# Strassen's form in the second product for four pairs of a chunk instead of two, in a kernel of channel attention and a gated network

## The chip, the cores and the metric

The program runs on one core of a Trainium2 chip. What is measured is device time in microseconds (us) of one execution; lower is better. Each engine of the core has an instruction stream of its own: PE (TensorE, the matrix products), ACT (ScalarE), DVE (VectorE), POOL (GpSimd) and SP, whose queue here issues nearly all DMAs. PSUM has 8 banks of 128 partitions by 512 float32; the products land there.

## The reference

For each of 4 batches, q, k and v are 6080 x 256. The columns of q and k are normed over the 6080 rows, a 256 x 256 attention between channels is formed, and `v @ a` goes through a network with 2048 hidden units.

```python
qn = q / (np.linalg.norm(q, axis=1, keepdims=True) + 1e-06)
kn = k / (np.linalg.norm(k, axis=1, keepdims=True) + 1e-06)
s = kn.transpose(0, 2, 1) @ qn / tau
a = np.exp(s - s.max(-1, keepdims=True))
a /= a.sum(-1, keepdims=True) + 1e-09
x = (v @ a).astype(np.float32).reshape(B * S, D)
h = x @ w_in
g = h * (1.0 / (1.0 + np.exp(-1.702 * h)))
return (g @ w_out).astype(np.float32)
```

## The kernel before

The kernel folds the attention of a batch into the network's first matrix (`a @ w_in`, once a batch), so that per token only two products are left: the **first product** (256 inputs to 2048 hidden units) and, behind the gate, the **second product** (2048 hidden units back to 256 outputs). Tokens lie along the free axis. A batch's 6080 tokens are cut into 6 **chunks**, five of 1024 and one of 960 columns; each has a left and a right half of 512 (or 480) columns. There are 24 chunks in all. Odd batches run their chunks backwards.

The 2048 hidden units are 8 **pairs** of 2 x 128. One pair in one chunk is a **unit** (`unit`); 192 units. To keep float32's accuracy with the fast float32r matmuls every operand is split into a high and a low part, and every product of two blocks is three matmuls: high x high, high x low, low x high. The split is a cast on ACT (`cast`, L299) or on DVE (`cast_v`, L302) and a subtraction on DVE (`low`, L310). Other two-operand work on DVE is `tt` (L305).

The first product of a unit is a 2x2 block product (two blocks of inputs, two of hidden units, two halves of columns) in Strassen's form (Winograd's variant): 7 block products of 3 matmuls, 21 instead of 24. They go to the banks X (two in turn), Y and Z, and copies on ACT and sums on DVE put the results together (`snap`, `add`, L966 for the matmuls). The gate (`gate`, L982) is on ACT.

The second product of a unit is done in one of two ways. **Plain** (L1046): the gated halves h1 and h2 are split (`split`: two casts and two lows of 1024 columns) and 8 block products, 24 matmuls, are added up in four banks O0 to O3 over the pairs of the chunk. **Joint** (`Joint`, L904), for two pairs (6 and 7, `MS = PAIRS = 2`), in each chunk but the first: the gates of both pairs write to tiles `g_a` and `g_b`, four sums of 1024 columns are formed on DVE (t1, t2, t3, t4), seven parts are split (7 casts, 7 lows of 1024 columns), and 7 block products of 2 pairs x 3 matmuls, 42 instead of 48, go to O0, O1 and O2. O1 is used for four products in turn (P1, P6, P5, P3); between them ACT copies what it holds to the output tile `osb` (`snap` in `products`). A split part is held in one of four tiles `gh` with its `gl` (`gh_slot`), taken in turn by the order in which the code asks for them, by joint parts and plain splits alike. The weights of the joint products are formed once and loaded again in each chunk as `w_oj`, four loads; the plain ones as `w_o`; both share four tiles (`NWO = 4`). The first product's weights `w_op` (896 KB a unit) have three. `values` splits a chunk's v into seven operands `v_op` of 512 columns; three of them (P1, P2, P6) have two tiles, the others one.

In the first chunk of a batch, and all through batches 0 to 2, the next batch's attention is worked in: loads of q and k, squares (ACT) and their sums `acc` (DVE), split of q and k (`qks`), the scores (PE, 256 columns), and at the end of the batch the next weights. The last batch has none of it.

What sets the order: `Plan` collects all instructions with dependencies, a cost, and a due time (45 units of time for each unit, plus an offset from the table `DUE` for its kind), runs a list scheduler over the engines, and emits the instructions in the order that comes out. Each engine then works through its own list strictly in that order.

In the joint chunks the pairs run in the order 6, 7, 0, 1, 2, 3, 4, 5:

```python
            joint = b > 0 or c > 0
            p = (x - MS) % NU if joint else x
```

## Time and profile before

| | |
|---|---|
| median of 3 runs (lowest, highest) | 2142.53 us (2141.75, 2144.03) |
| the profiled execution | 2142.41 us |
| its span, first to last instruction | 2140.6 us |
| TensorE clock granted, mean | 0.998 of full |
| busy: PE, DVE, ACT | 2131.3, 1659.3, 1409.6 us |
| matmul records, DVE and ACT instructions | 9774, 2199, 2078 |
| DMA | 448.32 MB, 209 GB/s over the span |

The profile is of one execution. Busy time of an engine is the time in which at least one of its instructions ran; matmuls overlap, so the mean duration of one (388 ns) is longer than the distance from one to the next. "PEld" is the load of weights, which runs beside the matmuls. In the lists of waits, the engine named first waited for the one behind the arrow. Some matmul records can be missing.

### The profile page before, as it was taken

The page shows a single profiled execution, that of the slowest core. Times are in us where ns is not written, and L with a number is a line of the kernel's source. Part 1 is how long each engine was busy: PE and PEld are TensorE (multiplying, and loading weights), DVE is VectorE, ACT ScalarE, POOL GpSimd, SP SyncE. Part 2 cuts the span into 40 slices and gives each one's busy share as a digit, 9 for nine tenths or more (in the row PEclk, how much of TensorE's full clock was granted, in tenths as well). Part 3 has the DMA queues.
Part 4 walks back from the last instruction along what each step waited for, and adds up shares of the span by engine and source line. Part 5 has one row for each costly group of instructions (what it writes and reads, how often), then busy time and mean ns, then how long its engine had stood idle before and what let it go on. Part 6 is the DMA issues. An engine that isn't in the chain of part 4 may idle for free.

```text
span 2140.6 us, 26818 instructions
## 1 busy us (share of the span) xinstructions
PE 2131.3 (100%) x9774; PEld 1785.7 (83%) x9774; DVE 1659.3 (78%) x2199; ACT 1409.6 (66%) x2078; POOL 6.4 (0%) x10
## 2 busy tenths in 40 slices
PE   9999999999999999999999999999999999999999
PEld 8888888888888888888888888888888888888887
DVE  6898888787778787867888878787787676676664
ACT  5568777666667676666766667666676565665663
POOL 0000000000000000000000000000000000000000
PEclk9999999999999999999999999999999999999999
DMA  9867666656765555555676556555577554554541
GB/s 342 307 216 284 236 246 217 218 176 219 258 243 200 188 204 192 207 172 180 245 255 211 189 197 211 182 202 173 183 251 256 187 201 150 201 180 160 195 170 74
DMA packets 124099, 448.32 MB, mean 209 GB/s; under 512 B 13120, under 2 KB 17344, under 8 KB 123968
## 3 DMA queue, kind: packets, MB, share of 16 engines
q1 hardware_dynamic: 123824, 446.48, 59.3%
q8 instruction: 77, 1.26, 0.2%
q14 instruction: 54, 0.44, 0.1%
q10 hardware_dynamic: 144, 0.13, 0.0%
HBM read 385.22 MB, written 61.34 MB: 209 GB/s over the span
## 4 chain that ended last, share of the span: by engine, by line
PE 98%; DMA 1%; ACT 0%; SPq 0%; issue 0%; DVE 0%; ACTq 0%
PE ps_o L1046 37%; PE ps_X L966 24%; PE ps_Y L966 12%; PE ps_o L904 10%; PE ps_Z L966 6%; PE ps_s L535 4%; PE ps_s L541 3%; PE ps_w L718 2%; DMA out_T<-osb 1%; DMA raw_qk<-in_q 0%; PE ps_n L595 0%; ACT osb L299 0%; PE ps_t L667 0%; SPq L296 0%; ACT gh L299 0%
## 5 line engine op out<-in xcount | busy, mean ns | idle before, releaser
L1046 PE MATMUL ps_o<-gh,w_o 128*128 128x512 f32 (+1 forms) x2336 | 716.6, 388 | 0.0
L966 PE MATMUL ps_X<-v_op,w_op 128*128 128x512 f32 (+1 forms) x2304 | 628.8, 389 | 0.6 <-ACT u L299 0.6
L1046 PEld LDWEIGHTS ps_o<-gh,w_o 128*128 128x128 f32 x2336 | 436.7, 188 | 86.8
L966 PEld LDWEIGHTS ps_X<-v_op,w_op 128*128 128x128 f32 x2304 | 430.3, 188 | 88.1 <-ACT u L299 1.4
L310 DVE TENSOR_TENSOR gl<-h,gh 128x1024 fp32r<-128x1024 f32 (+1 forms) x292 | 354.2, 1213 | 149.0 <-ACT gh L299 137.8
L1046 PE MATMUL ps_o<-gl,w_o 128*128 128x512 f32 (+1 forms) x1168 | 452.7, 388 | 0.0
L299 ACT COPY s<-ps_X 128x512 f32<-128x512 f32 (+1 forms) x384 | 222.7, 580 | 215.4 <-PE ps_X L966 142.3
L966 PE MATMUL ps_Y<-v_op,w_op 128*128 128x512 f32 (+1 forms) x1152 | 322.6, 388 | 0.0
L982 ACT ACTIVATE h<-h 128x512 f32<-128x512 f32 (+3 forms) x292 | 240.0, 838 | 58.8 <-DVE h L305 58.4
L1046 PEld LDWEIGHTS ps_o<-gl,w_o 128*128 128x128 f32 x1168 | 219.2, 188 | 43.9
L966 PEld LDWEIGHTS ps_Y<-v_op,w_op 128*128 128x128 f32 x1152 | 214.9, 188 | 42.8 <-DVE h L305 0.8
L904 PE MATMUL ps_o<-gh,w_oj 128*128 128x512 f32 (+1 forms) x644 | 222.2, 388 | 1.2 <-ACT osb L299 1.2
L299 ACT COPY u<-ps_X 128x512 f32<-128x512 f32 (+1 forms) x192 | 111.1, 578 | 119.3 <-DVE h L305 70.1
L299 ACT CAST gh<-h 128x1024 fp32r<-128x1024 f32 (+1 forms) x154 | 160.5, 1042 | 38.6 <-PE ps_o L904 25.7
L966 PE MATMUL ps_Z<-v_op,w_op 128*128 128x512 f32 (+1 forms) x576 | 161.0, 388 | 0.0
L302 DVE CAST gh<-h 128x1024 fp32r<-128x1024 f32 (+1 forms) x138 | 94.5, 685 | 80.5 <-PE ps_o L1046 59.1
L904 PEld LDWEIGHTS ps_o<-gh,w_oj 128*128 128x128 f32 x644 | 120.9, 188 | 26.6 <-ACT osb L299 2.5
L305 DVE TENSOR_TENSOR h<-ps_Y,s 128x512 f32<-128x512 f32 (+1 forms) x146 | 99.3, 680 | 44.8 <-ACT s L299 35.9
L305 DVE TENSOR_TENSOR h<-ps_Z,s 128x512 f32<-128x512 f32 (+1 forms) x146 | 99.2, 680 | 37.6 <-ACT s L299 17.2
L305 DVE TENSOR_TENSOR acc<-acc,sq 128x1024 f32<-128x1024 f32 (+2 forms) x96 | 112.8, 1175 | 18.4 <-ACT sq L502 16.6
L966 PEld LDWEIGHTS ps_Z<-v_op,w_op 128*128 128x128 f32 x576 | 107.7, 188 | 21.2
L904 PE MATMUL ps_o<-gl,w_oj 128*128 128x512 f32 (+1 forms) x322 | 124.8, 388 | 0.0
(110 smaller groups left out, 2281.3 us busy)
## 6 DMA issues: line engine op xcount, KB each, us to landing
w_op<-w_ops SPq DMA_DIRECT2D x184, 896.0 KB, 5.3
w_o<-wo_ops SPq DMA_DIRECT2D x138, 512.0 KB, 3.6
w_oj<-wj_ops SPq DMA_DIRECT2D x69, 512.0 KB, 3.8
raw_qk<-in_q SPq DMA_DIRECT2D x114, 256.0 KB, 5.4
raw_qk<-in_k SPq DMA_DIRECT2D x114, 256.0 KB, 5.5
w_ops<-w_op SPq DMA_DIRECT2D x32, 896.0 KB, 5.5
v_raw<-in_vT SPq DMA_DIRECT2D x20, 1024.0 KB, 6.8
out_T<-osb SPq DMA_DIRECT2D x39, 512.0 KB, 5.5
```

Source lines behind the costliest of these rows:

```text
L299: return g.add("ACT", act(n, psum), lambda: nc.scalar.copy(dst(), src()), deps, uses, due)
L302: return g.add("DVE", dve_fast(n), lambda: nc.vector.tensor_copy(dst(), src()), deps, uses, due)
L305: return g.add("DVE", dve(n), lambda: nc.vector.tensor_tensor(dst(), a(), b(), op=op), deps, uses, due)
L310: lambda: nc.vector.tensor_tensor(dst(), src(), hi().bitcast(F32), op=ALU.subtract),
L535: nc.tensor.matmul(out, lhsT=hl()[:pp, 1, j, ci], rhs=hl()[:pp, 0, j, :], start=begin, stop=last, skip_group_check=True,)
L541: nc.tensor.matmul(out, lhsT=hl()[:pp, 1, j, l, ci], rhs=hl()[:pp, 0, j, r, :], start=begin and m == 0, stop=last and m == 2, skip_group_c ...
L718: nc.tensor.matmul(pb()[:, x * width : (x + 1) * width], lhsT=aT()[:, l, j, ci], rhs=wi()[:, r, o : o + width], start=x == 0 and n == 0, s ...
L904: nc.tensor.matmul(of(into), lhsT=wt()[:, x, j, l, :], rhs=r()[:, j, :hw], start=begin and j == 0 and n == 0, stop=True, skip_group_check= ...
L966: nc.tensor.matmul(of(into), lhsT=wt()[:, m, l, :], rhs=v[m]()[:, r, :hw], start=begin and n == 0, stop=True, skip_group_check=True,)
L982: "ACT", act(n, psum), lambda: nc.scalar.activation(dst(), src(), AF.Gelu_apprx_sigmoid),
L1046: nc.tensor.matmul(of(ob), lhsT=wo()[:, l, i, ds], rhs=rr()[:, n * hw : (n + 1) * hw], start=first and m == 0, stop=True, skip_group_check ...
```

## The change

Four pairs (4 to 7) go in the joint form instead of two, as two groups of two pairs: group `b` in the table's names is pairs 6 and 7 (index 1), group `a` is pairs 4 and 5 (index 0). Each group has its own `g_a` and `g_b`; the products of both groups for one block are added in the same bank, so that each chunk has 14 parts, 8 sums and 84 joint matmuls, and 4 plain units. This holds from the third chunk of batch 0 on; the second chunk has the joint form for pairs 6 and 7 alone, as before, and the weights for pairs 4 and 5 are formed in it (`wout_later`, from a copy `wout_f` in DRAM). The joint pairs run first (4, 5, 6, 7, then 0 to 3). The weights `w_oj` come in seven loads of 512 KB, one for each block product, through the same four tiles. Of the plain units all four have the cast of h2 on DVE (before: all six); all joint casts are on ACT. `values` splits blocks of v that lie side by side together: P1 with P2, P5 with P7, P4 with P3, as one cast and one low of 1024 columns each (P6 alone); now only the first pair has two tiles. To make room, some tiles share a place that had one each: `wst`, `t2` and the words of small statistics go to `wa`, `sq` and one tile `few`, and the store of the next batch's weights is two DMAs instead of one. Every number of `DUE` is new, so the order of instructions changes everywhere.

```diff
 DUE = {
-    "m1": -16, "s1": -89, "m2": 50, "m6": 44, "u2": -64, "c11": -4, "g11": 193, "m5": 58, "u4": -39,
...
+    "m1": 17, "s1": -290, "m2": 48, "m6": 58, "u2": -133, "c11": -41, "g11": 708, "m5": 62, "u4": -220,
+    "m7": 67, "c22": -175, "m3": -16, "g12": -259, "m4": 71, "c21": -85, "g2": 1066, "h1": -392, "l1": 6,
...
 LAG = 3200
 NWO = 4
+MS = 4
+NV = {"m1": 2}
+NH = 2
+BY_V = (4, 5, 6, 7)
 
...
-    MS = PAIRS
     JOINT = list(range(NU - MS, NU))
-    wo_ops = dr.tile([NU - MS, P, 2, 2, C], F32, name="wo_ops")
-    wj_ops = dr.tile([P, NK, MS, 2, P], F32, name="wj_ops")
+    JG = MS // PAIRS
+    wo_ops = dr.tile([NU, P, 2, 2, C], F32, name="wo_ops")
+    wout_f = dr.tile([P, FG * C], F32, name="wout_f")
+    wj_ops = dr.tile([NK, P, MS, 2, P], F32, name="wj_ops")
...
+        if grp == NG - 1:
+            wout_sevens(grp, t, n, due + DUE["wj"], "acc")
+        elif PAIRS * grp in JOINT:
+            wo_stored["f"] = g.add("SP", 50 + 512 * 2.6, lambda: nc.sync.dma_start(wout_f, t()), [n], [t], due + 20, lag=LAG)
         return got
+
+    def wout_sevens(grp, t, ready, due, sums):
+
+        for a in range(PAIRS):
+            p = PAIRS * grp + a
+            view = lambda i, a=a: lambda: t()[:, (2 * a + i) * C : (2 * a + i + 1) * C].rearrange("p (d x) -> p d x", d=2)
+            wo_stored["joint", p] = sevens(
+                (t, view(0)), (t, view(1)), [ready], due + 20 * a, [("gA0", 0, NK)], sums,
+                lambda k, z, p=p: wj_ops[k:z, :, p - JOINT[0]].rearrange("k p h x -> p k h x"),
+            )[2]
+
+    def wout_later(grp, due, after):
+        t = sbuf("gB0", [P, FG * C], F32, "wf")
+        n = load(lambda: t(), wout_f, 512, [wo_stored["f"], *after], [t], due - 25)
+        wout_sevens(grp, t, n, due, "w1")
...
-    def wout_joint(due):
+    def wout_joint(due, pairs):
         got = {}
-        stored = [wo_stored["joint", p] for p in JOINT]
-        for x, (k, z) in enumerate(((0, 2), (6, 7), (4, 6), (2, 4))):
-            w = wo_tile([P, 2, MS, 2, P], "w_oj")
-            n = load(lambda w=w, k=k, z=z: w()[:, : z - k].bitcast(F32), wj_ops[:, k:z], 256 * (z - k), stored, [w], due + 8 * x)
-            for m in range(k, z):
-                got[m] = w, m - k, n
+        first = pairs[0] - JOINT[0]
+        stored = [n for p in pairs for n in wo_stored["joint", p]]
+        for x, m in enumerate((P1, P2, P6, P7, P5, P3, P4)):
+            w = wo_tile([P, MS, 2, P], "w_oj")
+            got[m] = w, load(
+                lambda w=w: w()[:, first:].bitcast(F32), wj_ops[m][:, first:], 128 * len(pairs), stored, [w], due + 8 * x,
+            )
         return got
...
-            v = sbuf(f"v{m}{turn if m in TWICE else ''}", [P, 2, HALF], F32R, "v_op")
-            at_ = due + 36 * n if m in TWICE else use + DUE[what] - 20
-            h = cast(lambda v=v: v()[:, 0, :hw], src, hw, [dep], [use_, v], at_)
-            ok[m] = low(
-                lambda v=v: v()[:, 1, :hw], src, lambda v=v: v()[:, 0, :hw], hw, [h], [use_, v], at_ + 6,
-            )
-            out[m] = v
...
+        def part(ms, what, src, n, deps, use_, at_):
+
+            k = len(ms)
+            v = sbuf(f"v{what}{turn % NV.get(what, 1)}", [P, 2, k, HALF], F32R, "v_op")
+            hi, lo = (lambda h=h: v()[:, h, :, :hw] if k > 1 else v()[:, h, 0, :hw] for h in range(2))
+            h = cast(hi, src, k * hw, deps, [use_, v], at_)
+            l = low(lo, src, hi, k * hw, [h], [use_, v], at_ + 6)
+            for i, m in enumerate(ms):
+                out[m] = v, lambda r, i=i, v=v: v()[:, r, i, :hw]
+                ok[m] = l
+            return l
+
+
+        col = lambda: raw()[:, :, :hw]
+        row = lambda j: lambda: raw()[:, j, : 2 * hw].rearrange("p (a n) -> p a n", a=2)
+        l1 = part((P1, P2), "m1", col, hw, [r], raw, due)
+        t1 = tt(B(0, 0), B(0, 1), B(0, 0), ALU.subtract, hw, [r, l1], [raw], due + 60)
+        t2 = tt(T2, B(1, 1), B(0, 0), ALU.subtract, hw, [t1], [raw, vt], due + 70)
+        t3 = tt(B(0, 1), B(0, 1), B(1, 1), ALU.subtract, hw, [t1], [raw], due + 80)
+        t4 = tt(B(1, 0), B(1, 0), T2, ALU.subtract, hw, [t2, l1], [raw, vt], due + 90)
+        part((P6,), "m6", T2, hw, [t2], vt, use + DUE["m6"] - 20)
+        part((P5, P7), "m5", row(0), hw, [t1, t3], raw, use + DUE["m5"] - 20)
+        part((P4, P3), "m3", row(1), hw, [t4], raw, use + DUE["m3"] - 20)
         return out, ok
...
+        def __init__(self, x, pairs):
+            self.x, self.pairs, self.ready = x, pairs, []
+            self.A = sbuf(f"gA{x}", [P, 2, len(pairs), HALF], F32, "g_a")
+            self.B = sbuf(f"gB{x}", [P, 2, len(pairs), HALF], F32, "g_b")
+
+    def joint_products(groups, b, c, due, wo):
...
+        for G in groups:
+            G11, G12, G2 = ([r[i] for r in G.ready] for i in range(3))
+            l1 = part(G, P1, "1", block(G.A, 0), G11, G.A)
+            l2 = part(G, P2, "2", block(G.B, 0), G2, G.B)
+            sums_[G.x] = G11, G12, G2, l1, l2
+        for G in groups:
...
+            t2 = sbuf("sq", [P, m_, HALF], F32, "g_t")
...
+            t1 = tt(B11, B12, B11, ALU.subtract, n_, [*G12, l1], [A], at("ta", G.x))
+            t2n = tt(T2, B22, B11, ALU.subtract, n_, [t1, *G2], [A, B_, t2], at("tb", G.x))
+            part(G, P6, "6", T2, [t2n], t2)
+            t4 = tt(B21, B21, T2, ALU.subtract, n_, [t2n, l2], [B_, t2], at("td", G.x))
+            t3 = tt(B12, B12, B22, ALU.subtract, n_, [t1, *G2], [A, B_], at("tc", G.x))
+            sums_[G.x] = G2, t1, t3, t4
+        for m, what, tile_, i, dep in (
+            (P7, "7", "A", 1, 2), (P5, "5", "A", 0, 1), (P3, "3", "B", 1, 0), (P4, "4", "B", 0, 3),
+        ):
+            for G in groups:
+                t = getattr(G, tile_)
+                dep_ = sums_[G.x][dep]
+                part(G, m, what, block(t, i), dep_ if isinstance(dep_, list) else [dep_], t)
+
...
+        def product(m, what, into, begin, deps):
+            ns = []
+            wt, w_ok = wo[m]
+            for G in groups:
+                gh, gl, ok = parts_[m, G.x]
+                m_ = len(G.pairs)
+
+                def fn(G=G, gh=gh, gl=gl, m_=m_):
                     for j in range(m_):
                         for n, (l, r) in enumerate(((0, gh), (0, gl), (1, gh))):
                             nc.tensor.matmul(
-                                of(into), lhsT=wt()[:, x, j, l, :], rhs=r()[:, j, :hw],
-                                start=begin and j == 0 and n == 0, stop=True, skip_group_check=True,
+                                of(into), lhsT=wt()[:, PAIRS * G.x + j, l, :], rhs=r()[:, j, :hw],
+                                start=begin and G is groups[0] and j == 0 and n == 0, stop=True, skip_group_check=True,
                             )
 
...
+                ns.append(g.add(
+                    "PE", 3 * m_ * width_cost(hw), fn, [*deps, ok, w_ok, *ns], [gh, gl, wt, into], at("q" + what, G.x), kind=hw,
+                ))
+            return ns[-1]
+
...
         r1 = split(h1, [g11, g12], "1", cast)
-        r2 = split(h2, [g2], "2", cast if D < NU else cast_v)
+        r2 = split(h2, [g2], "2", cast_v if D >= NU and x % NU in BY_V else cast)
...
-            joint = b > 0 or c > 0
-            p = (x - MS) % NU if joint else x
+            joint = JOINT if b > 0 or c > 1 else JOINT[-PAIRS:] if c > 0 else []
+            order = joint + [p for p in range(NU) if p not in joint]
+            p = order[x]
             grp, a = divmod(x, PAIRS)
...
             if joint and x == 0:
-                J = Joint(JOINT)
-                wj = wout_joint(due + DUE["wa"])
-            if joint and x >= MS:
+                Js = []
+                wj = wout_joint(due + DUE["wa"], joint)
+            if x < len(joint) and a == 0:
+                Js.append(Joint((p - JOINT[0]) // PAIRS, [p, p + 1]))
+            if joint and p not in joint:
                 wos[p] = wout_again(p, due + DUE["wb"])
-            unit(W, V[b, c], b, c, p, x, None if joint and x < MS else wos[p], J if joint and x < MS else None)
-            if joint and x == MS - 1:
-                J.products(b, c, due, wj)
+            unit(W, V[b, c], b, c, p, x, None if p in joint else wos[p], Js[-1] if p in joint else None)
+            if b == 0 and c == 1 and x == 3:
+                wout_later(JOINT[0] // PAIRS, due + 20, [marks[-1]])
+            if joint and x == len(joint) - 1:
+                joint_products(Js, b, c, due, wj)
...
```

How the order moves is shown at three places, all in the last batch's third chunk or, for the queue of DMAs, its last. `gh`, `gl` are a part's high and low half, `w_oj` the weights of joint products, `ps_o`, `ps_X`, `ps_Y`, `ps_Z` the banks.

PE, before: what stands between the last plain product of the chunk before and the joint product P7, whose part takes over the same `gh` and `gl` tile (the first row reads the old part, the last one the new one).

```order
L1046 MATMUL ps_o_15575<-gl_15859,w_o_15691 128x512
L966 MATMUL ps_X_16012<-v_op_15213,w_op_15948 128x512 x3
L904 MATMUL ps_o_16021<-gh_15906,w_oj_15771 128x512
L904 MATMUL ps_o_16021<-gl_15918,w_oj_15771 128x512
L904 MATMUL ps_o_16021<-gh_15906,w_oj_15771 128x512 x2
L904 MATMUL ps_o_16021<-gl_15918,w_oj_15771 128x512
L904 MATMUL ps_o_16021<-gh_15906,w_oj_15771 128x512
L966 MATMUL ps_Y_15993<-v_op_15779,w_op_15786 128x512 x3
L966 MATMUL ps_X_15940<-v_op_15264,w_op_15863 128x512 x3
L966 MATMUL ps_Z_16044<-v_op_15220,w_op_15863 128x512 x3
L904 MATMUL ps_o_16049<-gh_16028,w_oj_15937 128x512
```

Between these two rows stand 18 matmuls.

PE, after: what stands between the product P2 of the second group and P7 of the second group, whose part takes over P2's tile (neither is in the rows).

```order
L1015 MATMUL ps_X_16169<-v_op_15804,w_op_16072 128x512 x3
L1015 MATMUL ps_X_16250<-v_op_15297,w_op_16166 128x512 x3
L950 MATMUL ps_o_16118<-gh_16134,w_oj_16053 128x512
L950 MATMUL ps_o_16118<-gl_16138,w_oj_16053 128x512
L950 MATMUL ps_o_16118<-gh_16134,w_oj_16053 128x512 x2
L950 MATMUL ps_o_16118<-gl_16138,w_oj_16053 128x512
L950 MATMUL ps_o_16118<-gh_16134,w_oj_16053 128x512
L950 MATMUL ps_o_16118<-gh_16238,w_oj_16053 128x512
L950 MATMUL ps_o_16118<-gl_16248,w_oj_16053 128x512
L950 MATMUL ps_o_16118<-gh_16238,w_oj_16053 128x512 x2
L950 MATMUL ps_o_16118<-gl_16248,w_oj_16053 128x512
L950 MATMUL ps_o_16118<-gh_16238,w_oj_16053 128x512
```

Again 18 matmuls, of which 12 are joint. Before, P7 was the only joint part of the chunk with fewer than 20 matmuls ahead of it in this way; now five of the 14 have 18 to 21 (P7 of the second group, P5 and P4 of both).

DVE, before: in the same chunk, from the first joint part's low on: the four sums (L305 from and to `g_a`, `g_b`, `g_t`) and the second part's low.

```order
L310 TENSOR_TENSOR gl<-g_a,gh 128x1024
L305 TENSOR_TENSOR g_b<-ps_Y,s_15900 128x512
L305 TENSOR_TENSOR g_a<-g_a 128x1024
L310 TENSOR_TENSOR v_op<-v_t,v_op 128x512
L305 TENSOR_TENSOR g_b<-ps_Y,u_15876 128x512
L305 TENSOR_TENSOR h_15960<-ps_Z,s_15929 128x512
L305 TENSOR_TENSOR g_a<-g_a,g_b 128x1024
L310 TENSOR_TENSOR gl<-g_b,gh 128x1024
L305 TENSOR_TENSOR g_t<-g_b,g_a 128x1024
L305 TENSOR_TENSOR osb<-ps_o,osb 128x512
L305 TENSOR_TENSOR g_b<-g_b,g_t 128x1024
```

DVE, after: the sums of the second group (the first group's stand some 15 rows ahead), with lows of both groups' parts between them.

```order
L312 TENSOR_TENSOR g_a<-g_a 128x1024
L312 TENSOR_TENSOR h_16184<-ps_Z,s_16136 128x512
L312 TENSOR_TENSOR g_a<-g_a,g_b 128x1024
L317 TENSOR_TENSOR gl<-g_b,gh 128x1024
L312 TENSOR_TENSOR h_16214<-ps_Y,s_16197 128x512
L312 TENSOR_TENSOR g_t<-g_b,g_a 128x1024
L317 TENSOR_TENSOR gl<-g_b,gh 128x1024
L312 TENSOR_TENSOR h_16214<-ps_Y,u_16181 128x512
L317 TENSOR_TENSOR gl<-g_t,gh 128x1024
L317 TENSOR_TENSOR gl<-g_a,gh 128x1024
L312 TENSOR_TENSOR h_16273<-ps_Z,s_16226 128x512
L312 TENSOR_TENSOR g_b<-g_b,g_t 128x1024
```

Where one set of four sums and seven lows stood among the first-product sums (`h`, `g_b` from `ps_Y`, `ps_Z`), two sets follow each other.

SP, before: the last chunk's loads of joint weights, among `w_op`, the plain `w_o` and the stores of output.

```order
L296 DMA w_oj<-wj_ops 128x1024
L296 DMA w_op<-w_ops 128x1792
L296 DMA w_oj<-wj_ops 128x512
L296 DMA w_op<-w_ops 128x1792
L296 DMA w_oj<-wj_ops 128x1024
L296 DMA w_op<-w_ops 128x1792
L296 DMA w_oj<-wj_ops 128x1024
L1082 DMA out_T<-osb 128x1024 x2
L296 DMA w_op<-w_ops 128x1792
```

SP, after: the same place.

```order
L303 DMA w_oj<-wj_ops 128x1024
L303 DMA w_op<-w_ops 128x1792 x2
L303 DMA w_oj<-wj_ops 128x1024
L303 DMA w_op<-w_ops 128x1792
L303 DMA w_oj<-wj_ops 128x1024
L303 DMA w_op<-w_ops 128x1792
L1131 DMA out_T<-osb 128x1024
L303 DMA w_oj<-wj_ops 128x1024 x2
L303 DMA w_op<-w_ops 128x1792
L1131 DMA out_T<-osb 128x1024
L303 DMA w_op<-w_ops 128x1792
L303 DMA w_oj<-wj_ops 128x1024 x2
```

Four loads of `w_oj` became seven, and the last three of them wait until one of the first four tiles is read out; the two halves of the output store are now parted by two loads of `w_oj` and one of `w_op`.

## Rows read from the trace of the kernel before

**Rows 1.** Part 1 of the page: busy us (share of span) xinstructions.

```profile
PE 2131.3 (100%) x9774; PEld 1785.7 (83%) x9774; DVE 1659.3 (78%) x2199; ACT 1409.6 (66%) x2078; POOL 6.4 (0%) x10
```

**Rows 2.** Part 4 of the page: the chain that ended last, by engine.

```profile
PE 98%; DMA 1%; ACT 0%; SPq 0%; issue 0%; DVE 0%; ACTq 0%
```

**Rows 3.** Waits of PE, whole span: us in total, times, longest.

```profile
PE ps_s L535 <- DMA raw_qk<-in_q: 2.0, 1, 2.0
PE ps_o L904 <- ACT osb L299: 1.2, 2, 0.8
...
PE ps_X L966 <- ACT u L299: 0.6, 1, 0.6
```

**Rows 4.** Groups by shape, PE: xcount, busy us, mean ns, idle before.

```profile
L904 PE MATMUL ps_o<-gh,w_oj 128*128 128x512 f32 x532 | 184.4, 390 | 1.2 <-ACT osb L299 1.2
...
L904 PE MATMUL ps_o<-gh,w_oj 128*128 128x480 f32 x112 | 37.8, 379 | 0.0
```

**Rows 5.** Timeline of PE, last batch: start us, us, line, xcount.

```profile
1764.71 0.84 PE L966 MATMUL ps_X<-v_op,w_op 128*128 128x512 f32 x3
...
1787.84 0.84 PE L966 MATMUL ps_Y<-v_op,w_op 128*128 128x512 f32 x3
...
1682.48 0.37 PE L904 MATMUL ps_o<-gh,w_oj 128*128 128x480 f32 x1
...
1685.73 0.38 PE L904 MATMUL ps_o<-gh,w_oj 128*128 128x480 f32 x1
```

**Rows 6.** Windows: length; each engine's busy us; PEclk, DMA share, GB/s.

```profile
756.00:840.00 84.00, 84.00 (x411) 71.17 (x410) 72.32 (x84) 59.24 (x82) 0.00 (x0) 1.00 0.57 200
...
1764.00:1848.00 84.00, 84.00 (x372) 69.54 (x371) 57.99 (x72) 50.29 (x74) 0.00 (x0) 1.00 0.50 181
```

**Rows 7.** Timeline of DVE, back to back, at 800 us.

```profile
799.51 1.21 DVE L310 TENSOR_TENSOR gl<-g_a,gh 128x1024 fp32r<-128x1024 f32 x1
800.65 1.22 DVE L310 TENSOR_TENSOR gl<-g_b,gh 128x1024 fp32r<-128x1024 f32 x1
...
809.62 0.68 DVE L305 TENSOR_TENSOR h<-ps_Z,s 128x512 f32<-128x512 f32 x1
810.22 0.68 DVE L305 TENSOR_TENSOR osb<-ps_o,osb 128x512 f32<-128x512 f32 x1
```

**Rows 8.** Groups by shape, DVE, then ACT, columns as in Rows 4.

```profile
L310 DVE TENSOR_TENSOR gl<-h,gh 128x1024 fp32r<-128x1024 f32 x244 | 298.7, 1224 | 126.5 <-ACT gh L299 117.4 <-DVE gh L302 0.5
...
L302 DVE CAST gh<-h 128x1024 fp32r<-128x1024 f32 x114 | 78.7, 691 | 67.0 <-PE ps_o L1046 47.9 <-ACT h L982 9.6 <-PE ps_o L904 8.9
...
L299 ACT CAST gh<-h 128x1024 fp32r<-128x1024 f32 x130 | 136.6, 1051 | 30.9 <-PE ps_o L904 19.1 <-PE ps_o L1046 9.9
...
L299 ACT CAST v_op<-v_raw 128x512 fp32r<-128x512 f32 x120 | 72.2, 621 | 31.0 <-PE ps_Y L966 11.9 <-PE ps_X L966 10.9 <-DMA v_raw<-in_vT 6.9
...
L299 ACT COPY osb<-ps_o 128x512 f32<-128x512 f32 x79 | 46.2, 585 | 35.9 <-PE ps_o L1046 24.2 <-PE ps_o L904 6.6 <-DMA out_T<-osb 4.6
```

**Rows 9.** Timeline, last batch: a cast behind PE, a low behind a cast.

```profile
1910.69 0.39 PE L904 MATMUL ps_o<-gh,w_oj 128*128 128x512 f32 x1
...
1911.11 1.06 ACT L299 CAST gh<-g_a 128x1024 fp32r<-128x1024 f32 x1 [0.70 <-PE ps_o L904]
...
2095.36 1.06 ACT L299 CAST gh<-h 128x1024 fp32r<-128x1024 f32 x1
...
2096.45 1.23 DVE L310 TENSOR_TENSOR gl<-h,gh 128x1024 fp32r<-128x1024 f32 x1 [3.01 <-ACT gh L299]
```

**Rows 10.** Part 6 of the page: DMA issues, KB each, median us to landing.

```profile
w_op<-w_ops SPq DMA_DIRECT2D x184, 896.0 KB, 5.3
...
w_oj<-wj_ops SPq DMA_DIRECT2D x69, 512.0 KB, 3.8
```

203 lines of the change are left out of this document (87 added, 116 removed), and 10 rows, old and new, of the table DUE.

## The prediction

> **What bounds the kernel now.** I read the shares of busy time first. PE is busy 2131.3 of 2140.6 us, DVE 78% and ACT 66% of the span [rows 1]. A busy share alone does not say that PE never waits, so the chain of work that ended last comes next: 98% of it is PE [rows 2]. Then the waits of PE: 2.0 us for the first q, 1.2 us for two copies out of the joint bank, 0.6 us for one other copy, and nothing else of note [rows 3]. So between start and end PE runs through without gaps, and the time is the number of matmuls times their distance, plus some 4 us at the end. The distance is to be read from starts, not from the mean duration of a record (390 ns), since matmuls overlap: in the last batch 102 matmuls of 512 columns start between 1764.71 and 1787.84, that is 226.8 ns each, and 15 of 480 columns between 1682.48 and 1685.73, 216.7 ns each [rows 5]. Last I looked at how full DVE is by stage, because the change loads it: 72.3 of 84 us where the next batch's attention is worked in, 58.0 of 84 in the last batch [rows 6].
>
> The profiled execution took 2142.41 us, 0.1 us under the median of the three runs, and 1.8 us of it lie outside the span. I sum against it. About 0.2% (4.3 us) is what a measurement of this kernel can tell from no change.
>
> **What is removed: matmuls.** A joint block of two pairs takes 42 matmuls where two plain units take 48. Two more pairs go joint in 22 chunks (all but the first two), so 22 x 6 = 132 matmuls go. In 4 of the 22 the halves have 480 columns: before, 23 chunks had 28 `gh` matmuls each, 532 of 512 columns (19 chunks) and 112 of 480 (4 chunks) [rows 4], and the two chunks that get nothing are of 1024 columns. So 108 x 0.2268 + 24 x 0.2167 = 24.5 + 5.2 = **29.7 us**, if PE stays full. The built order bears the count out: 9558 matmuls become 9426, 108 and 24 fewer by width. All of it lies on the path, since PE does.
>
> The Trainium skill, "TensorE: Matmul & The Clock Gate", section "Back-to-back issue gap", states another distance for a sustained stream at 512 columns, about 131 ns. By it the 132 would bring 17.3 us and the time would be 2125, an estimate from that page. The rows of this case have 226.8 ns over 102 matmuls [rows 5], so I give that figure no chance.
>
> **What is added: work on DVE and ACT.** Per chunk with four joint pairs: splits go from 12 + 7 to 8 + 14 lows, sums from 4 to 8, so 7 more DVE instructions of 1024 columns. Back to back they start 1.14 us apart, those of 512 columns 0.60 us [rows 7]. Two casts of 0.69 us leave DVE [rows 8]. The splitting of v trades six lows of 512 for three of 1024: 6 x 0.60 - 3 x 1.14 = 0.2 us saved. DVE: 7 x 1.14 - 1.4 - 0.2 = +6.4 us. ACT: casts of the second product go from 13 to 18, +5 x 1.05, and v from 6 x 0.62 to 3 x 1.05, together +4.7 us [rows 8]. Against the stage tables that is, in the fullest stretch, 72.3 + 6.4 = 78.7 us of DVE in 82.6 us of PE (95%), ACT 63.9 (77%); in the last batch DVE 64.4 of 82.6 (78%) [rows 6]. So neither becomes the bound by sheer amount. It costs nothing as long as PE's work covers it; without that cover the 6.4 us would come back 16 times in the chunks with attention.
>
> **New waits of PE on a split part.** A part's `gh` tile is filled again only when its last matmul is through. I took the refill from four rows: the cast begins 0.42 us after the last matmul that reads the old part starts, which is 0.2 us after that matmul's slot is over; it takes 1.06, the low begins 0.03 us behind a cast and takes 1.23 [rows 9]; with some 0.1 us to PE, 2.6 us. Then I counted in the built orders, at the distances of [rows 5], what PE has to do between a tile's old and new part. Before: 24 refills have under 4.8 us, nearly all of them P7 with 18 matmuls (4.1 us), and PE did not wait for a `gl` once [rows 3]. After: 66 refills have under 4.8 us, 40 under 4.1 and 13 under 3.5, shortest 2.7. With nothing queued ahead none waits: 0 us, the lower end. With one 1024-column instruction ahead on DVE (1.14) a refill takes 3.7 and the 13 lose 0.3 us each: 4 us. With one ahead on ACT too (1.05) it takes 4.8: 13 x 1.4 + 27 x 0.7 = 37 us, the upper end. I take **+3 us**, close to the row that shows none, because before's P7 is the same situation, and a little above it because DVE is fuller.
>
> **The shared bank.** P1, P6, P5 and P3 use bank O1 in turn, and ACT must copy it out between them. PE waited 1.2 us for it in all [rows 3]. Before, 25 of the 69 hand-overs have only 6 matmuls or so (1.36 us) of other work, after 10 of 66, because the second group's product stands in between. So I take **-1.2 us**; the range for it is -1.2 to +1. The Trainium skill speaks against such a bank: "Perfetto Trace Analysis", section "Optimizing Tensor Performance", wants independent groups of matmuls to rotate through different PSUM banks. It is a rival below; the trace so far shows the cost at 1.2 us.
>
> **Edits taken at nothing.** (1) Seven loads of `w_oj` through four tiles: a load lands in 3.8 us, with an `w_op` of 5.3 us ahead at worst [rows 10]. P3's load may start when P2's tile is read out, and from there the last batch's order has 51 matmuls (11.6 us) to P3's first; P4's has 39 (8.8 us). Uncovered, each of the three would cost up to its 3.8 us. (2) Blocks of v split in pairs with one tile: at the change of chunk the tile is read out, cast and subtracted (2.6 us as above) while PE has at least 4.5 us and mostly 6 to 7 us of other work. (3) Memory traffic grows by some 21 MB (85 loads of 512 KB more and 16 of 256 KB fewer of `w_oj`, 44 fewer of `w_o`) on 448 MB; the DMA share is 0.57 in the fullest DVE stretch [rows 6]. (4) The first chunk: the 1 MB of `w_in` words goes ahead of the first q instead of 1 MB of `w_out` words; same bytes, and DVE has a little less there (it forms pairs 4 and 5's joint weights one chunk later). (5) The end: the last 72 matmuls and what follows stand as before. Each of these is bounded by -1 and +2 us.
>
> **Sum.** 2142.4 - 29.7 - 1.2 + 3 = **2114.5 us**. With no new waits it is 2111.5; the floor is a little below that, 2109, for 0.1% between executions.
>
> **The rivals.**
>
> *DVE falls behind in the 16 chunks with attention: 2126.* By the order, in the first chunk of batch 1, DVE has some 30 us of instructions (at mean durations such as those in [rows 8]) between the sums of bank Z of two units that stand two apart, and PE 12 us between the same units' products for Z; that is 18 us more, and before the widest such bulge was 9 us more (31 against 22). For it: 95% full, and a strict order. Against it: the following unit has 20 us of PE and 10 of DVE, so the bulge has room. Price: one refill a chunk that meets both queues, 0.7 us, or 16 x 0.7 = 11 us on top.
>
> *The burst does not fit, slower: 2161.* If the 22 lows and sums of the two groups came only after the fourth unit's gate, DVE would need 22 x 1.14 + 6 x 0.60 + 4 x 1.14 of attention = 33.2 us, while PE has 84 joint matmuls, two units of first products (42) and 12 score matmuls, 30 us at most. The missing 3 us and more in 16 chunks are about 50 us. It decides from 2 us a chunk on (31 / 16). Against it: in the order 9 of the 22 stand ahead of the last sum of the fourth joint unit, which is 10 us of the 25, and first products of four units lie between the joint ones.
>
> *The bank's hand-over binds, no change or slower: 2147.* A copy takes 0.58 us [rows 8]; with an ACT instruction of 1.05 us ahead a hand-over takes 1.9 us, 0.55 more than 6 matmuls cover. All 66 at that price are 36 us. For it: ACT gets fuller. Against: only 10 of the 66 are that short, and 25 such before cost 1.2 us.
>
> *The paired split of v is late: 2135.* One cast now waits for two products; 1 us in each of 23 changes of chunk. Against: cover of 4.5 us and more.
>
> **How the numbers follow.** Forecast 0.68, DVE late 0.20, burst 0.06, bank 0.03, v 0.03. The likeliest case gives 2114.5. The forecast with its bounds spans 2109 to 2120; reaching over the middle of the second case leaves out the rest of it and the last three: 2109 to 2129. Faster by over 0.2% (below 2138.2): 0.68 + 0.20 + 0.03 = 0.91; the bank case lies at the edge, so same 0.02 and slower 0.07.
>
> **What would show it.** Right: 132 fewer matmul records, the joint line with twice its count; DVE busy near 1659 + 22 x 6.4 = 1800 us, ACT near 1513; PE's list of waits under 8 us in all, with `gl` at its head; distances still 226.8 ns at full clock. Wrong: windows of 84 us in batches 0 to 2 in which PE is busy 82 us or less with DVE above 80 (second or third case); PE waiting for `osb` (bank), for `v_op` (v), or for a DMA of `w_oj` (loads). If the loss sits in the last batch as well, where DVE has room, it is not DVE's amount.

## The result, and the profile after

The changed kernel takes **2121.34 us** (median of 4 runs, 2119.37 to 2123.15); the kernel before, on the same chip, 2142.14 (2138.66 to 2144.03). The ratio is 0.9905, 95% interval 0.9887 to 0.9922: 20 us faster. The forecast was 2114.5 with a range of 2109 to 2129, so direction and range held, and 6.8 us of the expected gain did not come. The profiled execution is the slowest of the four, 2123.15 us.

The page of the changed kernel, parts 1 and 4, to be held against [rows 1] and [rows 2]:

```profile
PE 2106.7 (99%) x9642; PEld 1760.3 (83%) x9642; DVE 1793.7 (85%) x2249; ACT 1507.2 (71%) x2124; POOL 7.5 (0%) x10
...
PE 93%; DMA 3%; DVE 2%; ACT 1%; issue 0%; SPq 0%; ACTq 0%; DVEq 0%
```

132 matmul records are gone, DVE has 134 us more and ACT 98. PE is idle for 2121.4 - 2106.7 = 14.7 us where it was idle for 9.3, and the chain of waits leaves PE for 7% of the span instead of 2%. Its waits, whole span (in total, times, longest), beside [rows 3]:

```profile
PE ps_X L1015 <- ACT u L306: 2.5, 3, 0.8
PE ps_s L556 <- DMA raw_qk<-in_q: 2.3, 1, 2.3
PE ps_X L1015 <- ACT s L306: 1.1, 3, 0.7
...
PE ps_o L950 <- ACT osb L306: 1.0, 1, 1.0
PE ps_o L950 <- DVE gl L317: 0.9, 2, 0.5
PE ps_o L950 <- DMA w_oj<-wj_ops: 0.5, 1, 0.5
```

The largest new one is neither `gl` nor the shared bank O1 but **bank X**, in which the first product adds up: 3.6 us against 0.6. The distance of matmuls is what it was [rows 5]: in the last batch 185 matmuls of 512 columns start between these two rows of the timeline, 226.6 ns each.

```profile
1743.34 0.84 PE L1015 MATMUL ps_Y<-v_op,w_op 128*128 128x512 f32 x3
...
1785.27 0.39 PE L1095 MATMUL ps_o<-gl,w_o 128*128 128x512 f32 x1
```

A list of waits shows only part of a late start, since a matmul's record (390 ns) reaches over the next one's place. So I went through the starts of all matmuls and took from each distance the usual one (226.7 ns at 512 columns, 216.7 at 480). What is over I call the **stretch**, and put it down to what the late matmul needs. Stretch at bank X: 3.0 us before, 8.6 after. At a joint product's `gl`: 0 and 1.8. At a joint product's bank or weights: 2.1 and 2.5. In the first 20 us, where PE waits for q: 10.0 and 10.7, but that part lies between 8.6 and 11.0 in the executions below, so nothing is read from it. The two profiled executions differ by 2142.41 - 2123.15 = 19.3 us, so all stretch together grew by some 10.5 us (29.7 - 19.2, the difference of the spans): 7.8 of it are the three named (5.6, 1.8 and 0.4), the rest is the start and small pieces.

The stage of [rows 6] after, and the loads of [rows 10]:

```profile
756.00:840.00 84.00, 83.54 (x400) 69.94 (x399) 73.61 (x81) 58.50 (x77) 0.00 (x0) 1.00 0.61 208
```

```profile
w_op<-w_ops SPq DMA_DIRECT2D x184, 896.0 KB, 5.0
w_oj<-wj_ops SPq DMA_DIRECT2D x154, 512.0 KB, 3.5
```

DVE is at 73.6 of 84 us there, not at the 78.7 that I had put together: the new order spreads the attention's work.

### The profile page after: what moved, and what is told of

Read it like the earlier page. It is cut to its first block, busy times and chain, and to the rows that moved or that the text cites. A ratio compares the mean times of both kernels' runs of the same rounds, so it can differ in the third digit from the quotient of the medians.

```text
span 2121.4 us, 26644 instructions
## 1 busy us (share of the span) xinstructions
PE 2106.7 (99%) x9642; PEld 1760.3 (83%) x9642; DVE 1793.7 (85%) x2249; ACT 1507.2 (71%) x2124; POOL 7.5 (0%) x10
## 4 chain that ended last, share of the span: by engine, by line
PE 93%; DMA 3%; DVE 2%; ACT 1%; issue 0%; SPq 0%; ACTq 0%; DVEq 0%
PE ps_o L1095 25%; PE ps_X L1015 23%; PE ps_o L950 19%; PE ps_Y L1015 11%; PE ps_Z L1015 6%; PE ps_s L556 4%; PE ps_s L562 3%; PE ps_w L739 2%; DMA out_T<-osb 1%; DMA raw_qk<-in_k 1%; DVE gl L317 1%; ACT gh L306 1%; DMA w_op<-w_ops 0%; DMA w_ops<-w_op 0%; DMA words<-in_w_out 0%
## 5 line engine op out<-in xcount | busy, mean ns | idle before, releaser
L1095 PE MATMUL ps_o<-gh,w_o 128*128 128x512 f32 (+1 forms) x1632 | 500.9, 388 | 0.0
L950 PE MATMUL ps_o<-gh,w_oj 128*128 128x512 f32 (+1 forms) x1260 | 420.5, 388 | 1.6 <-ACT osb L306 1.0
L1095 PEld LDWEIGHTS ps_o<-gh,w_o 128*128 128x128 f32 x1632 | 304.9, 188 | 60.1
L1095 PE MATMUL ps_o<-gl,w_o 128*128 128x512 f32 (+1 forms) x816 | 316.3, 388 | 0.0
L950 PE MATMUL ps_o<-gl,w_oj 128*128 128x512 f32 (+1 forms) x630 | 244.6, 388 | 0.9 <-DVE gl L317 0.9
L1031 ACT ACTIVATE h<-h 128x512 f32<-128x512 f32 (+2 forms) x204 | 170.3, 841 | 29.7 <-DVE h L312 28.7
L317 DVE TENSOR_TENSOR gl<-g_a,gh 128x1024 fp32r<-128x1024 f32 (+1 forms) x135 | 162.2, 1209 | 21.6 <-ACT gh L306 20.1
L317 DVE TENSOR_TENSOR gl<-g_b,gh 128x1024 fp32r<-128x1024 f32 (+1 forms) x135 | 162.4, 1208 | 10.7 <-ACT gh L306 10.5
L306 ACT CAST gh<-g_a 128x1024 fp32r<-128x1024 f32 (+1 forms) x135 | 141.1, 1045 | 29.0 <-PE ps_o L950 20.1
L306 ACT CAST gh<-g_b 128x1024 fp32r<-128x1024 f32 (+1 forms) x135 | 140.7, 1045 | 19.4 <-PE ps_o L950 13.4
```

Source lines behind the costliest of these rows:

```text
L306: return g.add("ACT", act(n, psum), lambda: nc.scalar.copy(dst(), src()), deps, uses, due)
L317: lambda: nc.vector.tensor_tensor(dst(), src(), hi().bitcast(F32), op=ALU.subtract),
L950: nc.tensor.matmul(of(into), lhsT=wt()[:, PAIRS * G.x + j, l, :], rhs=r()[:, j, :hw], start=begin and G is groups[0] and j == 0 and n == 0 ...
L1031: "ACT", act(n, psum), lambda: nc.scalar.activation(dst(), src(), AF.Gelu_apprx_sigmoid),
L1095: nc.tensor.matmul(of(ob), lhsT=wo()[:, l, i, ds], rhs=rr()[:, n * hw : (n + 1) * hw], start=first and m == 0, stop=True, skip_group_check ...
```

## The experiments

Each run was timed beside the kernel before on the same chip, in three rounds of four runs (in the order of the rows behind the changed kernel) on three chips, where the kernel before took 2142.71, 2142.48 and 2141.86. Stretch is from one profiled execution of each, in us. The last column is the time from the first product into X to the end of the span in that execution. That product starts between 78.3 and 82.1 us in these executions, and the spread is there already at the 224th score matmul, 20.8 us ahead of it in each of them; the two executions of the changed kernel alone are 0.9 us apart in it. Behind it the two executions of the changed kernel agree within 0.4 us (2121.4 - 82.1 and 2120.1 - 81.2), so a row's last column, though from one execution, tells smaller differences than its median. Three of these rows, of the changed kernel, `after_again` and `mended`:

```profile
82.11 0.86 PE L1015 MATMUL ps_X<-v_op,w_op 128*128 128x512 f32 x3
```

```profile
81.19 0.86 PE L1015 MATMUL ps_X<-v_op,w_op 128*128 128x512 f32 x3
```

```profile
78.79 0.86 PE L1069 MATMUL ps_X<-v_op,w_op 128*128 128x512 f32 x3
```

| run | median (lowest to highest) | ratio to before, 95% | stretch at X | at `gl` | from the first X on |
|---|---|---|---|---|---|
| changed kernel | 2121.34 (2119.37 to 2123.15) | 0.9905 [0.9887, 0.9922] | 8.6 | 1.8 | 2039.3 |
| after_again | 2120.53 (2117.90 to 2124.00) | 0.9899 [0.9882, 0.9916] | 9.2 | 0.9 | 2038.9 |
| pe_later | 2125.31 (2121.49 to 2128.44) | 0.9921 [0.9907, 0.9934] | 6.2 | 4.9 | 2040.2 |
| act_first | 2120.48 (2119.29 to 2121.20) | 0.9899 [0.9886, 0.9913] | 5.8 | 2.3 | 2037.5 |
| both | 2123.34 (2121.10 to 2123.80) | 0.9911 [0.9897, 0.9925] | 4.2 | 5.4 | 2041.0 |
| dve_light | 2120.13 (2118.41 to 2122.97) | 0.9897 [0.9884, 0.9911] | 10.0 | 1.2 | 2041.0 |
| act_light | 2119.87 (2118.08 to 2121.18) | 0.9894 [0.9881, 0.9908] | 8.0 | 1.7 | 2038.0 |
| one_group | 2216.94 (2211.46 to 2222.75) | 1.0348 [1.0325, 1.0372] | 17.0 | 4.3 | 2134.2 |
| pool_acc | 2138.49 (2136.01 to 2141.29) | 0.9982 [0.9973, 0.9990] | 9.1 | 1.3 | 2058.4 |
| matmuls_back | 2148.95 (2145.64 to 2149.77) | 1.0030 [1.0018, 1.0041] | 7.5 | 1.3 | 2065.7 |
| later_dve_light | 2122.15 (2121.40 to 2122.56) | 0.9909 [0.9896, 0.9923] | 6.0 | 4.4 | 2041.0 |
| later_act_light | 2122.06 (2120.70 to 2122.81) | 0.9907 [0.9892, 0.9922] | 6.0 | 3.8 | 2041.4 |
| mended | 2120.52 (2117.12 to 2123.86) | 0.9902 [0.9888, 0.9915] | 6.2 | 1.6 | 2036.5 |

### Is it the hand-over of bank X?

One place shows the question. Timeline of the changed kernel, second batch, all engines but the weight loads:

```profile
898.14 1.06 ACT L306 CAST gh<-g_t 128x1024 fp32r<-128x1024 f32 x1
898.29 0.85 PE L1015 MATMUL ps_X<-v_op,w_op 128*128 128x512 f32 x3
...
898.99 0.85 PE L1015 MATMUL ps_Z<-v_op,w_op 128*128 128x512 f32 x3
899.10 1.04 ACT L306 CAST gh<-g_a 128x1024 fp32r<-128x1024 f32 x1
...
900.05 0.57 ACT L306 COPY u<-ps_X 128x512 f32<-128x512 f32 x1
...
900.68 0.96 PE L1015 MATMUL ps_X<-v_op,w_op 128*128 128x512 f32 x3 [0.84 <-ACT u L306]
```

PE works three matmuls for X (the last starts at 898.76) and three for Z, and could go on at 899.67, but the copy that lets go of X begins only at 900.05, behind a cast: PE starts 1.0 us late. Two things are against it: only 0.68 us of PE work between two uses of X, where a copy begins 0.43 us after the last matmul's start at best and takes 0.58; and the cast ahead on ACT. The built order has eight hand-overs of X with less than 0.9 us of other PE work, the kernel before one. In the trace these eight cost 4.7 us, and PE waited for six copies behind a 1.05 us instruction.

So my theory was A, that PE's order leaves X too little cover; the rivals are B, that the split parts come late and PE has nothing else that is ready, and C, ACT's queue. The control, unchanged, which came out as expected:

> The changed kernel as it is, to stand beside the others on the same chip. All theories: 2119 to 2123 us, PE's starts stretched by about 8.6 us in all at first products into bank X, 1.8 us at a joint product's gl.

`pe_later` and `act_first` reorder the finished list, each at its places alone, and `both` does the two (`n` is a product into X, the `m`-th of its unit, and `cover` the time of PE's work since the one before):

```diff
-        for n in g.order():
+        for n in pe_later(list(g.order())):
             n.fn()
...
+        if m:
...
+            cover = sum(x.cost for x in pe[k + 1 : i])
+            to = i
+            while cover < 900:
+                to += 1
+                cover += pe[to].cost
+            if to > i:
...
+                behind(L, n, pe[to])
```

> Edit: eight first products into bank X that have under 0.9 us of other PE work between them and the product before them in the same bank (0.68 us six times, 0.44 and 0 once) are put behind PE's next product; nothing else changes. Theory A (the order of PE leaves too little work between two uses of bank X; the hand-over itself takes 0.43 + 0.58 us): these eight cost 4.7 us in the trace, so 2117 us (2116 to 2118.5), and the stretch at bank X falls from 8.6 to about 4 us. Theory B (DVE is late with the burst of two groups, and PE has nothing ready): the product put ahead waits for its gl instead, 2121 us. Theory C (ACT's queue: casts of 1.05 us stand ahead of the copies): only the two places with a cast ahead gain, 2119 us.

```diff
+FIRST = ((0, 1), (76, 1), (92, 2), (98, 1), (124, 1), (145, 0))
...
+    for n in [n for n in L if n.tag and n.tag[0] == "copy" and n.tag[1:] in FIRST]:
+        ahead = [x for x in L[: L.index(n)] if x.eng == "ACT"][-1]
...
+        behind(L, ahead, n)
```

> Edit: at six copies out of bank X the ACT instruction of 1.05 us that stands right ahead of the copy is put behind it; nothing else changes. PE waited 1.1, 1.1, 1.1, 0.45, 0.45 and 0.1 us at these six. Theory C (ACT's queue): 3.5 us come back, 2118 us, and the stretch at bank X falls from 8.6 to about 5 us. Theory A (order of PE): at two of the six the cover is 0.68 us, so 0.4 us of each 1.1 stays; 2118.5 us. Theory B (DVE late): the casts put back delay a gl by as much as the copy gains, 2121 us.

> The two edits together: eight first products later on PE, six copies earlier on ACT. Theories A and C together: 4.7 us of the first, and 1.1 + 0.45 + 0.45 + 0.1 us that the first doesn't have, 6.8 us: 2114.5 us, the stretch at bank X under 2.5 us. Theory B: 2121 us, the waits turn up at gl.

`pe_later` came out slower than expected by any of the three, 2125.31, and `both` too, 2123.34 where A and C have 2114.5 and B 2121. In `pe_later` stretch at X fell by 2.4 us as it should, and at `gl` rose by 3.1. The same place there:

```profile
898.49 1.05 ACT L347 CAST gh<-g_b 128x1024 fp32r<-128x1024 f32 x1
...
899.76 0.86 PE L1056 MATMUL ps_X<-v_op,w_op 128*128 128x512 f32 x3
...
900.45 0.86 PE L1056 MATMUL ps_Z<-v_op,w_op 128*128 128x512 f32 x3
...
901.15 0.40 PE L991 MATMUL ps_o<-gh,w_oj 128*128 128x512 f32 x1
901.23 1.22 DVE L358 TENSOR_TENSOR gl<-g_t,gh 128x1024 fp32r<-128x1024 f32 x1
...
902.50 0.50 PE L991 MATMUL ps_o<-gl,w_oj 128*128 128x512 f32 x1 [0.95 <-DVE gl L358]
```

PE goes straight on to the joint product that now stands ahead, and waits for its `gl`: 1.1 us late instead of 1.0. Some of its waits, whole span:

```profile
PE ps_o L991 <- DVE gl L358: 2.7, 3, 1.0
...
PE ps_Y L1056 <- DVE h L353: 0.8, 1, 0.8
...
PE ps_o L1140 <- DVE gl L358: 0.5, 1, 0.5
PE ps_o L1140 <- ACT gh L347: 0.4, 1, 0.4
```

At six of the eight places another wait took the place of X. With the longer distance that follows a late start (last section) the two of 1.1 us became 1.2 and the one of 0.95 became 1.4, all three at a joint part's `gl` (the last one in part at its `gh`). The three in the first batch went from 0.8 together to 2.5, but not at a joint part: there PE waits for the sum on DVE that lets go of bank Y, and for a plain unit's `gh` and `gl` (L1140). Only two places were free (0.4 and 0.3 us). `act_first` took 2.8 us off X, of which 0.5 came back at `gl` and 0.8 at Y and Z; its median is that of the unchanged kernel, while from the first X on it is 1.4 to 1.8 us shorter. So theory A names the places, but what PE needs next is late at most of them too, which is the half of B that held; that DVE is why is a question of its own.

### Which engine makes the parts late?

`dve_light` leaves out three sums of each joint group, `act_light` the gates in place on joint pairs:

```diff
+            for t in (t1, t3, t4):
+                t.fn = lambda: None
             sums_[G.x] = G2, t1, t3, t4
```

> Leaves out three of the four subtractions that form the joint product's sums of blocks (the second, third and fourth), in every joint group: 43 groups x 3 = 129 DVE instructions of 1024 columns, 157 us of DVE at 1.22 us; the order of all that is left is that of the changed kernel. The first four runs said that PE's waits at bank X turn into waits for gl when PE's order is mended, so the parts come late. Theory B1 (DVE is the late engine in the chunk where two groups are split): most of the 10 us by which PE's starts are stretched more than before come back, 2112 us (2110 to 2115), stretch at X under 4 us, gl under 0.5. Theory B2 (ACT is the late engine): 2119 to 2121 us. Theory B3 (a chain that alternates between ACT and DVE): about half, 2116 us.

```diff
+            g11.fn = g2.fn = lambda: None
             joint.ready.append((g11, g12, g2))
```

> Leaves out the gates that ACT works in place on the joint pairs' blocks (the first block and the two of the second half; the one read from bank X stays): per chunk with four joint pairs 4 x 1.06 + 4 x 0.63 = 6.8 us of ACT, 146 us in all; the order of all that is left is that of the changed kernel. Theory B1 (DVE late): 2118 to 2121 us. Theory B2 (ACT late): 2112 us, stretch at X under 4 us. Theory B3 (alternating chain): about half or more, 2112 to 2116 us.

The pages' part 1 of `dve_light` and of `act_light`:

```profile
PE 2103.8 (99%) x9642; PEld 1758.4 (83%) x9642; DVE 1650.0 (78%) x2114; ACT 1504.5 (71%) x2124; POOL 7.4 (0%) x10
```

```profile
PE 2102.9 (99%) x9642; PEld 1759.1 (83%) x9642; DVE 1793.1 (85%) x2249; ACT 1370.8 (65%) x1944; POOL 7.5 (0%) x10
```

144 us less of DVE (135 instructions: there are 45 joint groups, not 43), 136 us less of ACT, each below what the kernel before had [rows 1]: and the time is 2120.13 and 2119.87, the unchanged kernel's. B1 fails in the run with the lighter DVE, B2 in the one with the lighter ACT, B3 in both. The eight short hand-overs cost 4.7 and 4.8 us in them as before, place by place the same (1.1 us at 898 in each). That cost hangs on the order on PE and, where a cast stands ahead of the copy, on ACT, and not on how full the engines are. So I put the two edits together, later products and a lighter engine:

> The eight first products put later on PE, and the three subtractions left out of each joint group (157 us less DVE work, sums of blocks wrong). Apart, neither gave anything: the first moved the waits from bank X to gl, the second left the eight hand-overs of bank X as they were, 4.7 us. Theory D (at these places two limits stand side by side: the hand-over of bank X, fixed by the order, and the next part, late through DVE): only together do they give, about 4 us, so 2116 to 2117 us, gl under 1.5 us. Theory E (the next part is late through ACT's casts or the whole chain, not DVE): as with the first alone, gl near 4.9 us, 2121 to 2125 us.

> The eight first products put later on PE, and the gates worked in place on joint pairs left out (146 us less ACT work, values wrong). Theory D: gl stays near 4.9 us, 2121 to 2124 us. Theory E: gl falls under 1.5 us, 2115 to 2117 us. If both this and the run with less DVE work fall, the part is late through a chain that takes turns on the two engines.

Neither is faster than the changed kernel, 2122.15 and 2122.06; `gl` is at 4.4 and 3.8. D falls, and E in its simple form too. The place again, in `later_dve_light`:

```profile
897.99 1.05 ACT L347 CAST gh<-g_b 128x1024 fp32r<-128x1024 f32 x1 [0.77 <-PE ps_o L993]
...
898.95 1.05 ACT L347 CAST gh<-g_t 128x1024 fp32r<-128x1024 f32 x1
899.07 1.22 DVE L358 TENSOR_TENSOR gl<-g_b,gh 128x1024 fp32r<-128x1024 f32 x1 [0.59 <-ACT gh L347]
...
900.22 1.22 DVE L358 TENSOR_TENSOR gl<-g_t,gh 128x1024 fp32r<-128x1024 f32 x1
...
901.49 0.50 PE L993 MATMUL ps_o<-gl,w_oj 128*128 128x512 f32 x1 [0.59 <-DVE gl L358]
```

and in `later_act_light`:

```profile
898.16 1.05 ACT L347 CAST gh<-g_b 128x1024 fp32r<-128x1024 f32 x1 [0.77 <-PE ps_o L991]
...
901.66 0.50 PE L991 MATMUL ps_o<-gl,w_oj 128*128 128x512 f32 x1 [0.65 <-DVE gl L358]
```

In both, ACT stands idle for 0.77 us until PE's matmuls let go of a `gh` tile; then come two casts and two lows in turn, and PE has its `gl` 3.50 us after the first cast began, to the hundredth the same with DVE lighter and with ACT lighter. In `pe_later` itself the same way takes 4.01 us (898.49 to 902.50): ACT comes to the first cast without a pause, the second cast waits for its sum, and the first low stands behind other work of DVE. PE is 1.1 us late there, and 0.8 in both of these runs (0.76 and 0.81). So at this place 0.3 to 0.4 us of the 1.1 come from the other work of the two engines, and come back when either has less. What is left is the loop through the tile: PE frees one of four, cast, low, PE, with one part ahead on each engine. From the end of the last old matmul's place (0.2 us ahead of the cast, as in [rows 9]) to the `gl` it takes 3.7 us, which is what the prediction had put together for a refill with one instruction ahead on DVE, and PE has 2.9 us to do in between. This is read from the rows of this place (the same place of the next batch, at 1427 us, is like it); a fifth pair of `gh` and `gl` tiles, which would test it, was not tried, so for the other places it stays open.

### The price of the matmuls, and one part undone

```diff
-                        for m, (l, rr) in enumerate(((0, gh), (1, gh), (0, gl))):
+                        terms = [(0, gh), (1, gh), (0, gl)]
+                        if D >= 2 * NU and x == NU - 3 and 2 * i + n < 3:
+                            terms.append((0, gl))
+                        for m, (l, rr) in enumerate(terms):
```

> The price of the 132 matmuls by itself: in each of the 22 chunks one plain unit's second product adds its third term a second time for six of its eight sums (a result of its own), so 108 matmuls of 512 and 24 of 480 columns come back, and nothing else is added or moved. If PE's count sets the time and the stretched starts are a fixed cost of places, 29.7 us come on top: 2150 to 2151 us. If the time is partly set by late parts (DVE or ACT), the longer PE work gives them room, and it is 2140 to 2147 us.

2148.95, between the two forecasts, and 27.6 us over the 2121.35 of the eight executions of the changed kernel. From the first X on it is 26.4 and 26.8 us longer than the two profiled ones. So the matmuls cost nearly the 29.7 us of the sum. That some 2 or 3 us of room came back is at the edge of what the medians tell, but the trace has it too: stretch at X is 7.5 and at the joint bank 1.8. The Trainium skill's "TensorE: Matmul & The Clock Gate", section "Back-to-back issue gap", states about 131 ns a matmul at 512 columns, by which they would take 17.3 us, an estimate; this run has 209 ns each in the medians, and the rows above 226.6.

```diff
-MS = 4
+MS = 2
-            if b == 0 and c == 1 and x == 3:
+            if MS > PAIRS and b == 0 and c == 1 and x == 3:
```

> Undoes the second group: two of eight pairs joint as before, all else as in the changed kernel (paired split of v, loads of one product each, its table of numbers). 132 matmuls come back, 29.7 us; DVE and ACT lose what the second group added. Theory B (the parts of two groups come late): the 8 to 10 us of stretch go too, 2142 us (2140 to 2145). Theory A in its last form (it is the new table's order of PE, whatever the load): the order of this kernel has 13 hand-overs of bank X with under 0.95 us between them, so the stretch at X stays at 6 us or more, 2148 us. If a load or the paired v costs anything, it shows in the same number: 2145 us or more with waits for w_oj or v_op.

2216.94: both miss by far, though the stretch at X is over 6 us (17.0). The table of due times was made for two groups, and with one of them the order falls apart elsewhere. PE's waits, first row:

```profile
PE ps_o L950 <- ACT osb L306: 31.3, 23, 4.4
```

23 hand-overs of the shared bank O1 cost 1.4 us of waiting each. The longest is followed by a slow stretch besides:

```profile
1718.70 0.81 PE L1015 MATMUL ps_X<-v_op,w_op 128*128 128x480 f32 x3
1723.88 0.77 PE L950 MATMUL ps_o<-gh,w_oj 128*128 128x480 f32 x1 [4.37 <-ACT osb L306]
```

```profile
1721.00:1729.00 8.00, 5.12 (x14) 4.33 (x15) 1.89 (x3) 3.45 (x6) 0.00 (x0) 0.57 0.36 128
```

PE stood for 4.37 us, and the granted clock fell to its lower level, 1.2 GHz, from 1721.5 to 1728.4 us; matmuls of 480 columns start 400 ns apart there instead of 217. Between its start and its last microseconds this run has six more such stretches, of 3.4 us, the changed kernel none. The run says nothing on the second group's own price, but it shows what the bank's rival would have looked like. What keeps the changed kernel at 1.0 us is not shown: the second group's product between two uses of O1 may be a reason, but the kernel before has one group too and waited 1.2 us [rows 3].

### Two attempts at a better version

```diff
             self.acc_n = tt(a, a, add, ALU.add, w, [n, self.acc_n], [sq, acc], due + 4)
+            if self.b:
+                self.acc_n.fn = lambda: nc.gpsimd.tensor_tensor(a(), a(), add(), op=ALU.add)
```

> The additions of squares of batches 1 to 3 (54 of 1.16 us) are made by POOL, which is idle, instead of DVE; order as in the changed kernel. All is computed. Theory B1: DVE loses 62 us in the fullest chunks, 40% of what the run without subtractions takes away, so 2 to 4 us come back: 2118 us. Theory B2: 2121 us. If POOL slows DVE beside it, DVE's mean for 1024 columns rises above 1.22 us and the gain is eaten.

2138.49, which gives back nearly the whole gain. (72 additions moved, not 54; 66 of them have 1024 columns.) The late starts are now at what DVE makes: stretch at Y is 4.9 us where it was 0.7, at a plain unit's `gl` 4.2 where it was under 0.3. The last section has the reason.

`mended` is `pe_later` at the two free places and `act_first` at four:

```diff
+LATER = ((84, 3), (132, 3))
+FIRST = ((0, 1), (76, 1), (124, 1), (145, 0))
```

> A version meant to beat both, all computed: two of the eight products later on PE (the two after which the first attempt showed no new wait: 0.41 and 0.33 us), four of the six copies earlier on ACT (1.1, 0.7, 0.7 and 0.45 us, after what the cover of 0.68 us leaves of the two in the middle). If each place keeps what it showed in the runs before, 3.6 us: 2117 us, which is at the edge of what the medians can tell from the changed kernel; the stretch at bank X falls from 8.6 to about 5 us with gl still under 2.

In its trace stretch at X is 6.2 us (the two places of 1.1 us are at 0.26) and at `gl` 1.6, as expected, but 2120.52 (2117.12 to 2123.86) cannot be told from the changed kernel's 2121.35. From the first X on it takes 2036.5 us, 2.4 and 2.8 less than the two executions of the changed kernel, where 3.6 were expected. So the trace has two thirds of the gain or more; the start, which lies 2.4 and 3.3 us earlier here than in those two, is as large an effect in a total. With one execution the gain is not shown beyond doubt, and no other version was found that beats the changed kernel.

## Why the prediction was right, and where it was off

- **The count and the distance** held: 132 records, 226.6 ns, 29.7 us; putting them back cost 27.6.
- **Work on DVE and ACT**: +134 and +98 us, against 22 x 6.4 = 141 and 22 x 4.7 = 103. That it costs nothing by its amount is shown: with 144 us less of one or 136 us less of the other, in the same order of instructions, the time stays.
- **New waits on `gl`**, +3 taken: stretch there is 1.8 us (0.9 in the second execution). The size was about right, the reason "nearly none waits" too, but it does not head the list of waits, as I had said it would, and the list comes to 9.9 us where I had said under 8.
- **The shared bank**, -1.2 taken: it did not come. PE waits 1.0 us there, and the stretch at joint banks and weights went from 2.1 to 2.5.
- **The term that is missing** is bank X: +5.6 us (3.0 to 8.6), with no place in the sum. Against the forecast's terms, 5.6 more here, 1.2 less at `gl` and 1.6 more at the joint bank make 6.0 of the 6.8. The step that failed is the counting of covers: I counted in the built order what PE has to do between two uses of a `gh` tile and of O1, and not between two uses of X, since the code of the first product was untouched. But the table was new, so its order was new too. The same count would have shown eight hand-overs under 0.9 us (before: one), and the copy of 0.58 us [rows 8], begun 0.42 us behind a matmul's start [rows 9], the price, by estimate some 4 us. That this is a price and not only a place, one trace each of `act_first` and `mended` bears out: with 2.8 and 2.4 us less stretch at X they are 1.4 to 2.8 us shorter from the first X on.
- **Taken at nothing**: PE waited 0.5 us once for `w_oj`; not at all for a `v_op`; the start differs by less than executions do (the 224th score matmul starts at 60.0 us before, 61.3 and 60.4 after, 57.5 to 61.1 in the other runs).
- **The rivals.** DVE late (2126): the time came out halfway to it, but not for its reason, as `dve_light` shows; after the first 84 us no full window of 84 us has PE under 82.8 or DVE over 77. My last sign, a loss in the last batch as well, did not help: behind 1600 us the late starts come to only some 1.6 us, which would have left DVE's amount as a cause, and `dve_light` shows that it is none. The burst (2161) and the paired v (2135) did not happen. That the range held is in part luck: its upper half was there for a late DVE, and bank X filled it. The bank's rival named the right mechanism in the wrong bank: a copy of 0.58 us behind a cast of 1.05 us, with too little PE work between.

Left open is why the next part is late at each of the six places; at the one read closely two thirds of it are the loop through the four `gh` tiles, by its rows and not by a test.

## What to carry to other kernels

When a change rebuilds the order, count the cover at every hand-over of a bank or a tile in the new order, those of untouched code too, each against the copy's duration from the trace. An engine waiting at a hand-over may have nothing else that is ready: moving the wait away pays only where the work put ahead is ready, and the trace of the first attempt tells at which places that is. Less work on an engine that is 70 to 85% busy bought nothing here that the time shows; the waits hang on single chains of a few instructions. And where the start of a kernel varies by microseconds, compare traces from a point behind it.
